# Linear attention and a gated layer on one core: tiles for the group sums, and the block-diagonal product in two halves

## The chip, the cores and the metric

The kernel runs on one core of a Trainium2 chip. The metric is the time of one execution on the device in microseconds. The engines are named as in the profile: PE is TensorE (its weight loads are PEld), DVE is VectorE, ACT is ScalarE, POOL is GpSimd, SP is SyncE, which issues nearly all transfers.

## The reference

```python
# q, k, v: (8, 8, 576, 64); w_in: (512, 2048); w_out: (2048, 512)
kv = np.einsum('bhsd,bhse->bhde', k, v)
out = np.einsum('bhsd,bhde->bhse', q, kv)
rms = np.sqrt(np.mean(out * out, axis=-1, keepdims=True) + 1e-06)
x = out / rms * g_norm                      # then to (4608, 512)
h = x @ w_in
sp = np.maximum(h, 0.0) + np.log1p(np.exp(-np.abs(h)))
g = h * erf(sp)
y = g @ w_out                               # (4608, 512) float32
```

## The kernel before

**Groups, batches, units.** The 4608 tokens are handled in nine groups. Groups 0 to 7 take the first 512 of the 576 rows of one batch element each; the remaining 64 rows of all eight elements are gathered in `x_last` and make group 8. In a group `x` is held transposed (features on the partitions, 512 tokens along the free dimension). The 2048 hidden features are cut into 16 units of 128; four units are a batch (`BATCH`), so a group has four batches and batch m of the whole kernel belongs to group m // 4. For each unit `hidden` makes `h`, ScalarE takes Softplus and Erf of it, VectorE multiplies, and the product with `w_out` is summed over the units into four tiles of sums, `e`.

**Two ways of multiplying.** Groups 0 and 1 use plain fp32 matmuls (L691 for `h`, L520 for the output) for most of their units. From group 2 on (`FIRST` = 2) each operand is cut into fp32r parts, and a product is twelve fp32r matmuls into two PSUM tiles, `n_ps` (eight) and `m_ps` (four), in `product` (L462). Their results are joined when they are evicted: L834 and L445 for `h`, L440 or L775 and L445 for `e`. The parts of the weights are written to DRAM once, in group 1, and read back for each group, as `w_in_parts` and `w_out_parts` (L595).

**Attention in pieces.** While one group goes through the gated layer, the attention of the next is made, one pair of heads (`p`) in each batch, in six pieces with fixed places in the batch's order:

- `products`: the two heads' `kv` products and the transposes of `q` (L297, L305, L319), copies of the two diagonal blocks into `bd_kv` (L312), of the tail of `q` into `qT_last` (L315, for two pairs at once, so only where `p` is even) and of `qT` (L320)
- `apply`: the block-diagonal product, for the tail of 64 tokens into a corner of the `kv` bank (L324) and for the 512 tokens into `se_ps` (L325); the tail's result goes to `x_last` (L326); Square (L328)
- `halve` and `mean`: the squares are cut into two fp32r parts (L338, L339), and two matmuls with `mean_w` give the means (L346, L347); then Ln, Exp, Square on ScalarE (L358 to L360)
- `norm`: three operations on VectorE (L366, L369, L378), the last of which writes `x` and is the last reader of the product's bank; `split` cuts `x` into `x_forms` (L405, L408, L411)

The engines run each their own queue in the order in which the program issues the instructions (`manual_schedule`); a tile taken from a pool waits for the last user of the buffer that it takes. In the main loop (from batch 8 on) the pieces stand at `places = (0, 2, 3, 5, 6, 8)`: before unit 0, after units 1 and 2, after results 0, 1 and 3 of the batch before. Batch m computes its own `h` and the results (`result`) of batch m - 1. SP's order in a batch is `FETCH`: one or two loads of parts at each place, between them the loads of `q`, `k`, `v` and, at the end of a group, the four stores of the sums (L531).

**Buffers that the change touches.** The pool `wide` has two buffers, and these take them in turns, in this order: xT of group 0, xT of group 1, `x_high` and `x_both` of group 1, the sums of group 1 (L735), and then `h` of every batch from 8 on (L822). The pool `acc` has one, for the sums of group 0, `old_h` of group 1's last four units (L700), and the sums of groups 2 to 8 (L773). In PSUM eight banks are split into `ps_h` (two), `ps_o` (four) and `ps_at` (two); the attention takes its tiles of one bank from `ps_at`.

Of the kernel before, what the change touches and what calls it, by code (L numbers as in the profile page):

```python
# [60 lines left out]
def kernel(  # L61
# [25 lines left out]
    attp = ctx.enter_context(tc.tile_pool(name="attp", bufs=1))  # L87
    dram = ctx.enter_context(tc.tile_pool(name="dram", bufs=1, space=bass.MemoryType.DRAM))

    wide = ctx.enter_context(tc.tile_pool(name="wide", bufs=2, side="right"))  # L90

    room, early_room, low_room = (ctx.enter_context(ExitStack()) for _ in range(3))
    first_w = room.enter_context(tc.tile_pool(name="first_w", bufs=1, side="right"))
    gate = room.enter_context(tc.tile_pool(name="gate", bufs=7, side="right"))
    early = early_room.enter_context(tc.tile_pool(name="early", bufs=2))
    ps_at = ctx.enter_context(tc.tile_pool(name="ps_at", bufs=2, space=PSUM))
    ps_h = ctx.enter_context(tc.tile_pool(name="ps_h", bufs=2, space=PSUM))
    ps_o = ctx.enter_context(tc.tile_pool(name="ps_o", bufs=1, space=PSUM))

    ctx.enter_context(tc.manual_schedule())  # L100

# [167 lines left out]
    def attention(T, p, pools=None):  # L269

        st = {}

        halves = FIRST <= T < B
        bd = bd_kv[:, (T * NP + p) % 2, :]

        q_tail, o_tail = slice(P, 2 * P), slice(2 * P, 2 * P + R)

        def bank(name):
            pool, tag = (pools or {}).get(name, (ps_at, "at"))
            return pool.tile([P, G], FP32, name=name, tag=tag)  # L280

        def square_tile(name):

            if T == 0:
                return gate.tile([P, G], FP32, name=name, tag="h")
            return attp.tile([P, G], FP32, name=name, tag="qT")

        def products():

            kv_ps = st["kv"] = bank("kv_ps")  # L290
            ks, vs, qs = (x.pop((T, p)) for x in (k_sb, v_sb, q_sb))
            C = chunks(T)
            for c in range(C):
                rows = slice(0, S // C + (c < S % C))
                for i in range(2):
                    s = slice(i * D, i * D + D)
                    nc.tensor.matmul(  # L297
                        kv_ps[s, s],
                        lhsT=ks[rows, i, c],
                        rhs=vs[rows, i, c],  # L300
                        start=(c == 0),
                        stop=(c == C - 1),
                    )
            if p % 2 == 0:
                nc.tensor.transpose(kv_ps[:, q_tail], q_last[:, p // 2], ident)  # L305
            if p == NP - 2:
                for i in range(NP):
                    load_last(T + 1, i)
            st["qT"] = square_tile("qT")
            for i in range(2):  # L310
                s = slice(i * D, i * D + D)
                nc.vector.tensor_copy(out=bd[s, s], in_=kv_ps[s, s])  # L312
            if p % 2 == 0:
                tails[T] = attp.tile([P, P], FP32, name="qT_last", tag="t")
                nc.vector.tensor_copy(out=tails[T], in_=kv_ps[:, q_tail])  # L315
            st["tail"] = tails[T][:, p % 2 * R : p % 2 * R + R]
            qt_ps = bank("qt_ps")
            for j in range(J):
                nc.tensor.transpose(qt_ps[:, j * P : j * P + P], qs[:, j], ident)  # L319
            nc.scalar.copy(st["qT"], qt_ps)  # L320

        def apply():
            qT, o_ps, kv_ps = st["qT"], bank("se_ps"), st.pop("kv")
            nc.tensor.matmul(kv_ps[:, o_tail], lhsT=bd, rhs=st.pop("tail"), start=True, stop=True)  # L324
            nc.tensor.matmul(o_ps, lhsT=bd, rhs=qT, start=True, stop=True)  # L325
            nc.vector.tensor_copy(out=x_last[:, p, T * R : T * R + R], in_=kv_ps[:, o_tail])  # L326
            st["o"] = o_ps
            nc.scalar.activation(qT, o_ps, AF.Square)  # L328

        def square():  # L330
            st["o"], st["qT"] = x_last[:, p, :], square_tile("sq")
            nc.scalar.activation(st["qT"], st["o"], AF.Square)

        def halve():
            sq = st.pop("qT")
            hi = st["hi"] = attp.tile([P, G], FP32R, name="sq_hi", tag="rms_r")
            lo = st["lo"] = attp.tile([P, G], FP32R, name="sq_lo", tag="sq_lo")
            nc.vector.tensor_copy(out=hi, in_=sq)  # L338
            nc.vector.tensor_tensor(out=lo, in0=sq, in1=hi.bitcast(FP32), op=ALU.subtract)  # L339

        def mean(table=True):
            ms = st["ms"] = bank("ms_ps")
            if halves:


                nc.tensor.matmul(ms, lhsT=mean_w, rhs=st.pop("hi"), start=True, stop=False)  # L346
                nc.tensor.matmul(ms, lhsT=mean_w, rhs=st.pop("lo"), start=False, stop=True)  # L347
                u = square_tile("u")
            else:
                u = st.pop("qT")  # L350
                nc.tensor.matmul(ms, lhsT=mean_w.bitcast(FP32), rhs=u, start=True, stop=True)  # L351
            if T > 0:
                r = attp.tile([P, G], FP32, name="rms_r", tag="rms_r")
                exp_ln_table()
            else:
                r = gate.tile([P, G], FP32, name="rms_r", tag="s")
            st["u"], st["r"] = u, r
            nc.scalar.activation(r, ms, AF.Ln, bias=eps_col)  # L358
            nc.scalar.activation(r, r, AF.Exp, scale=-0.5)
            nc.scalar.activation(u, r, AF.Square)  # L360
            if table and (T > 0 or p == NP - 1):
                softplus_table()

        def norm():
            ms, u, r = (st.pop(name) for name in ("ms", "u", "r"))
            nc.vector.scalar_tensor_tensor(  # L366
                out=u, in0=ms, scalar=EPS, in1=u, op0=ALU.add, op1=ALU.mult
            )
            nc.vector.scalar_tensor_tensor(  # L369
                out=u, in0=u, scalar=3.0, in1=r, op0=ALU.subtract, op1=ALU.mult  # L370
            )
            if T < FIRST:
                if T not in xT:
                    xT[T] = wide.tile([P, KC, G], FP32, name="xT", tag="h")
                x = xT[T][:, p, :]
            else:
                x = st["x"] = x_new.tile([P, G], FP32, name="x", tag="x")
            nc.vector.scalar_tensor_tensor(  # L378
                out=x,
                in0=st.pop("o"),  # L380
                scalar=gm_col,
                in1=u,
                op0=ALU.mult,
                op1=ALU.mult,
            )

        def split():
            if T >= FIRST:
                thirds(st.pop("x"), *(form[:, p] for form in x_forms[T]))

        def loads():
            load_pair(T * NP + p + 2)

        if T == 0:
            return products, apply, halve, mean, norm
        if T == B:
            return lambda: None, square, lambda: None, mean, norm, split

        pieces = ((products,), (apply,), (halve, loads)) if halves else ((products, loads), (apply,), ())
        return (*(partial(chain, *group) for group in pieces), mean, norm, split)  # L400


# [241 lines left out]
    for n in range(FIRST * FC + 1):  # L644
        T, f = divmod(n, FC)
        if n == FC:
            early_room.close()
            late = ctx.enter_context(tc.tile_pool(name="late", bufs=1))
            x_new = ctx.enter_context(tc.tile_pool(name="x_new", bufs=1))
            acc = ctx.enter_context(tc.tile_pool(name="acc", bufs=1))  # L650
            w_in_p = ctx.enter_context(tc.tile_pool(name="w_in_p", bufs=BATCH))
            low = low_room.enter_context(tc.tile_pool(name="low", bufs=1))
            forms = late.tile([P, 3, KC, G], FP32R, name="x_forms0")
            x_forms[FIRST] = [forms[:, i] for i in range(3)]
# [13 lines left out]
            gates(done)  # L668
        if T == FIRST - 1:
            if f == 0:  # L670
                x_high = wide.tile([P, KC, G], FP32R, name="x_high", tag="h")
                x_low = low.tile([P, KC, G], FP32R, name="x_low")
                for i in range(0, KC, 2):
                    upper(xT[T][:, i : i + 2], x_high[:, i : i + 2])
# [23 lines left out]
        if T < FIRST:  # L698
# [8 lines left out]
                add(h, m_ps)  # L707
            if T == FIRST - 1:
                if f == 1:
                    x_both = wide.tile([P, KC, G], FP32R, name="x_both", tag="h")  # L710
                    for i in range(0, KC, 2):
                        both_only(x_high[:, i : i + 2], x_low[:, i : i + 2], x_both[:, i : i + 2])
                    x_forms[T] = x_high, x_low, x_both
# [16 lines left out]
        if n >= LAG:  # L730
# [1 line left out]
            last = n - LAG in (FC - 1, whole - 1)  # L732
            project(f2, hs[n - LAG], last)
            if last:
                sums(*((acc, "e") if T2 < FIRST - 1 else (wide, "h")))  # L735
                if T2 == 0:
                    for j in range(J):
                        store(T2, j, es.pop(j))
# [26 lines left out]
    def result(T, b, j, g, w):  # L765
# [4 lines left out]
        )  # L770
        if b == 0:
            if j == 0:
                all_e = acc.tile([P, J, DM], FP32, name="e", tag="e")  # L773
                es.update((i, all_e[:, i]) for i in range(J))
            nc.vector.tensor_scalar(  # L775
                out=es[j], in0=ps[0], scalar1=SHIFT - 1.0, scalar2=None, op0=ALU.mult
# [9 lines left out]
    for m in range(first_batch, batches + 1):  # L786
# [32 lines left out]
        g, done = g_next, len(g_next)  # L819
        g_next = []  # L820
        if m < batches:
            h = wide.tile([P, BATCH, G], FP32, name="h", tag="h")  # L822
            s = gate_r.tile([P, BATCH, G], FP32, name="s", tag="s")
        for i in range(BATCH):
            if m < batches:
# [68 lines left out]
```

## Time and profile before

| | |
|---|---|
| Median of 12 runs | 953.72 us (951.44 to 954.97) |
| The profiled execution | 953.61 us, its span 951.8 us |
| Granted TensorE clock, mean | 0.998 |
| PE busy | 929.3 us (98%), 4272 matmuls |
| DVE busy | 740.8 us (78%) |
| ACT busy | 616.1 us (65%) |
| DMA | 259.78 MB, 273 GB/s over the span |

The shares are of the span. The first 150 us hold the conversion of the weights and group 0, the next 105 us group 1; from 256 us on the main loop runs, 28 batches of about 25 us and a last round of results. The times in the views are microseconds from the start of the span.

### The profile page before, as it was taken

To read this page: it belongs to the slowest core of one execution; us is meant where nothing else is said; L and a number is where in the kernel's file an instruction comes from. 1 tells how busy PE (TensorE), PEld (TensorE's weight loads), DVE (VectorE), ACT (ScalarE), POOL (GpSimd) and SP (SyncE) were. 2 spreads that over 40 slices of the span, in tenths; PEclk is the share of its full clock that TensorE was granted. 3 is DMA by queue.
4 is the path that set the end of the run, shared out by engine and by line. 5 is a ranking of instruction groups with operands and counts; after the bars stand their busy time and mean duration, and the time that the engine had idled before them with its cause. 6 is when DMAs were issued, how large, how long until landed. Compare 5 with 4: busy or idle time off the path is not lost.

```text
span 951.8 us, 11746 instructions
## 1 busy us (share of the span) xinstructions
PE 929.3 (98%) x4272; PEld 684.7 (72%) x4272; DVE 740.8 (78%) x1054; ACT 616.1 (65%) x825; POOL 2.4 (0%) x10
## 2 busy tenths in 40 slices
PE   6999999999998999999999999999999999999998
PEld 4444445665686788888888888888888788878886
DVE  3979958888575888888888887887887877777667
ACT  3889876777665666666666666666666666665552
POOL 1000000000000000000000000000000000000000
PEclk9999999999999999999999999999999999999999
DMA  9756505899699878898889889988896778768872
GB/s 256 278 167 214 163 6 219 308 351 336 209 360 334 286 266 300 290 305 295 299 312 314 290 294 307 329 291 285 286 338 254 262 255 346 285 249 310 331 272 64
DMA packets 111842, 259.78 MB, mean 273 GB/s; under 512 B 43864, under 2 KB 69544, under 8 KB 111784
## 3 DMA queue, kind: packets, MB, share of 16 engines
q1 hardware_dynamic: 110152, 256.73, 77.7%
q10 hardware_dynamic: 1568, 2.29, 0.8%
q8 instruction: 34, 0.56, 0.2%
q14 instruction: 24, 0.20, 0.1%
q0 software_dynamic: 64, 0.00, 0.0%
HBM read 224.40 MB, written 34.60 MB: 272 GB/s over the span
## 4 chain that ended last, share of the span: by engine, by line
PE 84%; ACT 6%; DVE 6%; DMA 3%; issue 1%; SPq 0%; DVEq 0%
PE n_ps L462 43%; PE m_ps L462 21%; PE o_ps L520 8%; PE h_ps L691 3%; PE se_ps L325 3%; PE kv_ps L297 2%; PE qt_ps L319 2%; DMA out_dram<-e 1%; DMA w_in_parts<-w_in 1%; ACT w_e L215 1%; ACT L103 1%; DVE h L445 1%; ACT w_m L219 1%; DMA v_sb<-in_v_dram 1%; PE ms_ps L351 1%
## 5 line engine op out<-in xcount | busy, mean ns | idle before, releaser
L462 PE MATMUL n_ps<-x_forms,w_in_parts 128*128 128x512 f32 x896 | 234.8, 404 | 4.8 <-ACT h L834 3.3
L462 PE MATMUL n_ps<-w_out_parts,g_forms 128*128 128x512 f32 x928 | 231.3, 391 | 0.0
L462 PEld LDWEIGHTS n_ps<-x_forms,w_in_parts 128*128 128x128 f32 x896 | 167.5, 189 | 49.2 <-issue 9.6
L462 PEld LDWEIGHTS n_ps<-w_out_parts,g_forms 128*128 128x128 f32 x928 | 174.2, 188 | 38.4 <-issue 1.4
L836 ACT ACTIVATE s<-h 128x512 f32<-128x512 f32 x112 | 71.1, 635 | 180.8 <-DVE h L445 180.8
L445 DVE TENSOR_TENSOR h<-m_ps,h 128x512 f32<-128x512 f32 x116 | 79.9, 688 | 68.1 <-ACT h L834 48.7
L462 PE MATMUL m_ps<-w_out_parts,g_forms 128*128 128x512 f32 x464 | 124.2, 389 | 0.0
L462 PE MATMUL m_ps<-x_forms,w_in_parts 128*128 128x512 f32 x448 | 120.2, 390 | 0.0
L520 PE MATMUL o_ps<-w_out_sb,h_sb 128*128 128x512 f32 x224 | 100.8, 592 | 0.3 <-DVE h_sb L642 0.3
L462 PEld LDWEIGHTS m_ps<-w_out_parts,g_forms 128*128 128x128 f32 x464 | 87.1, 188 | 18.1
L462 PEld LDWEIGHTS m_ps<-x_forms,w_in_parts 128*128 128x128 f32 x448 | 84.4, 188 | 17.8
L445 DVE TENSOR_TENSOR e<-m_ps,e 128x512 f32<-128x512 f32 x116 | 80.3, 692 | 17.9 <-PE m_ps L462 10.5
L440 DVE SCALAR_TENSOR_TENSOR e<-n_ps,e 128x512 f32<-128x512 f32 x88 | 60.4, 686 | 37.5 <-PE n_ps L462 37.5
L520 PEld LDWEIGHTS o_ps<-w_out_sb,h_sb 128*128 128x128 f32 x224 | 42.3, 190 | 48.9 <-issue 46.6
L834 ACT ACTIVATE h<-n_ps 128x512 f32<-128x512 f32 x112 | 65.6, 586 | 13.3 <-DMA w_in_parts<-w_in 9.4
L411 DVE SCALAR_TENSOR_TENSOR g_forms<-g_forms 128x1024 fp32r<-128x1024 f32 x58 | 71.1, 1226 | 2.0
L408 DVE TENSOR_TENSOR g_forms<-h,g_forms 128x1024 fp32r<-128x1024 f32 x58 | 70.6, 1218 | 1.7 <-ACT g_forms L405 1.4
L405 ACT ACTIVATE g_forms<-h 128x1024 fp32r<-128x1024 f32 x58 | 58.9, 1060 | 12.4 <-PE m_ps L462 9.8
L854 DVE TENSOR_TENSOR h<-h,s 128x1024 f32<-128x1024 f32 x56 | 66.0, 1219 | 0.7 <-ACT s L840 0.7
L691 PE MATMUL h_ps<-xT,w_in_sb 128*128 128x512 f32 x144 | 65.0, 595 | 0.8 <-DVE w_in_sb L240 0.6
L106 ACT ACT_TABLE_LOAD x44 | 56.5, 1283 | 0.7
L840 ACT ACTIVATE s<-s 128x1024 f32<-128x1024 f32 x56 | 56.3, 1052 | 0.3
(98 smaller groups left out, 1015.3 us busy)
## 6 DMA issues: line engine op xcount, KB each, us to landing
w_out_parts<-w_out SPq DMA_DIRECT2D x116, 768.0 KB
w_in_parts<-w_in SPq DMA_DIRECT2D x112, 768.0 KB
w_in<-w_new SPq DMA_DIRECT2D x16, 768.0 KB
q_sb<-in_q_dram SPq DMA_DIRECT2D x32, 256.0 KB
w_raw<-in_moe_w_out_dram SPq DMA_DIRECT2D x8, 1024.0 KB
out_dram<-e SPq DMA_DIRECT2D x32, 256.0 KB
k_sb<-in_k_dram SPq DMA_DIRECT2D x28, 287.5 KB
v_sb<-in_v_dram SPq DMA_DIRECT2D x28, 287.5 KB
```

Of the source, the lines that this page charges most:

```text
L106: nc.scalar.preload_act_table_set("softplus")
L405: nc.scalar.activation(high, x, AF.Copy, scale=1.0 + 2.0**-13)
L408: nc.vector.tensor_tensor(out=low, in0=x, in1=high.bitcast(FP32), op=ALU.subtract)
L411: nc.vector.scalar_tensor_tensor(out=both, in0=low.bitcast(FP32), scalar=SHIFT, in1=high.bitcast(FP32), op0=ALU.mult, op1=ALU.add,)
L440: nc.vector.scalar_tensor_tensor(out=out_, in0=ps, scalar=scale, in1=out_, op0=ALU.mult, op1=ALU.add)
L445: nc.vector.tensor_tensor(out=out_, in0=ps, in1=out_, op=ALU.add)
L462: nc.tensor.matmul(ps, lhsT=weights(form, k), rhs=moving(form, k), start=(form == forms[0] and k == 0), stop=(form == forms[-1] and k == 3),)
L520: nc.tensor.matmul(o_ps[j], lhsT=g[:, j * P : j * P + P], rhs=w_out_sb[:, f, :], start=(f == 0), stop=last,)
L691: nc.tensor.matmul(plain[i], lhsT=w_in_sb[:, c, i % FC * P : i % FC * P + P], rhs=xT[T][:, c, :], start=(c == 0), stop=(c == KC - 1),)
L834: nc.scalar.activation(h[:, i], n_ps, AF.Copy, scale=SHIFT - 1.0)
L836: nc.scalar.activation(s[:, i], h[:, i], AF.Softplus)
L854: nc.vector.tensor_tensor(out=part(h, half), in0=part(h, half), in1=part(s, half), op=ALU.mult)
```

## The change

The two wide tiles now have a name each: "a" for xT of group 0, `x_high` and the sums of groups 1 to 8, "b" for xT of group 1, `x_both` and `h` of the even batches from 8 on. `h` of the odd batches takes the tile of `acc`. The attention pieces of group 2 and later get one PSUM tile of two banks (`ps_two`, where `ps_at` was). The tail of `q` is laid beside `qT`, so that each of two halves has 256 + 32 columns, and the block-diagonal product becomes two matmuls of 288 columns, one in each bank; the means take the columns from 256 on of both banks, in four matmuls of 256 columns. The transposes of `q` are issued ahead of the copies.

```diff
-    wide = ctx.enter_context(tc.tile_pool(name="wide", bufs=2, side="right"))
+    wide = ctx.enter_context(tc.tile_pool(name="wide", bufs=1, side="right"))
...
         def bank(name):
+            if T >= FIRST:
+                return two_banks()[:, name in ("qt_ps", "se_ps")]
...
+        def two_banks():
+            if "two" not in st:
+                st["two"] = ps_two.tile([P, 2, G], FP32, name="at_ps", tag="at")
+            return st["two"]
+        HG, HR = G // 2, R // 2
+        def twofold(x):
+            return x.rearrange("p (i n) -> p i n", i=2) if halves else x
...
+            t = attp.tile([P, 2, HG + HR], FP32, name=name, tag="qT")
+            if tail:
+                return t
+            return t[:, :, :HG] if halves else t.rearrange("p i n -> p (i n)")[:, :G]
...
+            qt_ps = bank("qt_ps")
+            for j in range(J):
+                nc.tensor.transpose(qt_ps[:, j * P : j * P + P], qs[:, j], ident)
             if p == NP - 2:
                 for i in range(NP):
                     load_last(T + 1, i)
-            st["qT"] = square_tile("qT")
+            st["qT"] = square_tile("qT", halves)
             for i in range(2):
                 s = slice(i * D, i * D + D)
                 nc.vector.tensor_copy(out=bd[s, s], in_=kv_ps[s, s])
-            if p % 2 == 0:
-                tails[T] = attp.tile([P, P], FP32, name="qT_last", tag="t")
-                nc.vector.tensor_copy(out=tails[T], in_=kv_ps[:, q_tail])
-            st["tail"] = tails[T][:, p % 2 * R : p % 2 * R + R]
...
-            nc.scalar.copy(st["qT"], qt_ps)
+            if halves:
+                tail = tails.pop(T) if p % 2 else kv_ps[:, P : P + R]
+                nc.vector.tensor_copy(out=st["qT"][:, :, HG:], in_=twofold(tail))
+                if p % 2 == 0:
+                    tails[T] = attp.tile([P, R], FP32, name="qT_next", tag="t")
+                    nc.vector.tensor_copy(out=tails[T], in_=kv_ps[:, P + R : 2 * P])
...
+            if halves:
+                nc.scalar.copy(st["qT"][:, :, :HG], twofold(qt_ps))
...
         def apply():
+            if halves:
+                qT, two = st.pop("qT"), two_banks()
+                del st["kv"]
+                for i in range(2):
+                    nc.tensor.matmul(
+                        two[:, i, : HG + HR], lhsT=bd, rhs=qT[:, i], start=True, stop=True
+                    )
+                nc.vector.tensor_copy(
+                    out=twofold(x_last[:, p, T * R : T * R + R]), in_=two[:, :, HG : HG + HR]
+                )
+                o_ps = st["o"] = two[:, :, :HG]
+                qT = st["qT"] = qT[:, :, :HG]
+                nc.scalar.activation(qT, o_ps, AF.Square)
+                return
...
-            ms = st["ms"] = bank("ms_ps")
+            ms = st["ms"] = two_banks()[:, :, HG:] if halves else bank("ms_ps")
             if halves:
-                nc.tensor.matmul(ms, lhsT=mean_w, rhs=st.pop("hi"), start=True, stop=False)
-                nc.tensor.matmul(ms, lhsT=mean_w, rhs=st.pop("lo"), start=False, stop=True)
+                hi, lo = (twofold(st.pop(name)) for name in ("hi", "lo"))
+                for i in range(2):
+                    nc.tensor.matmul(ms[:, i], lhsT=mean_w, rhs=hi[:, i], start=True, stop=False)
+                    nc.tensor.matmul(ms[:, i], lhsT=mean_w, rhs=lo[:, i], start=False, stop=True)
...
-                    xT[T] = wide.tile([P, KC, G], FP32, name="xT", tag="h")
+                    xT[T] = wide.tile([P, KC, G], FP32, name="xT", tag="ab"[T])
...
+            at_room.close()
+            ps_two = ctx.enter_context(tc.tile_pool(name="ps_two", bufs=1, space=PSUM))
...
-                x_high = wide.tile([P, KC, G], FP32R, name="x_high", tag="h")
+                x_high = wide.tile([P, KC, G], FP32R, name="x_high", tag="a")
...
-                    x_both = wide.tile([P, KC, G], FP32R, name="x_both", tag="h")
+                    x_both = wide.tile([P, KC, G], FP32R, name="x_both", tag="b")
...
-                sums(*((acc, "e") if T2 < FIRST - 1 else (wide, "h")))
+                sums(*((acc, "e") if T2 < FIRST - 1 else (wide, "a")))
...
-                all_e = acc.tile([P, J, DM], FP32, name="e", tag="e")
+                all_e = wide.tile([P, J, DM], FP32, name="e", tag="a")
...
-            h = wide.tile([P, BATCH, G], FP32, name="h", tag="h")
+            pool, tag = (acc, "e") if m % 2 else (wide, "b")
+            h = pool.tile([P, BATCH, G], FP32, name="h", tag=tag)
```

`halves` is true for groups 2 to 7. VectorE's and ScalarE's operations on `qT`, `hi`, `lo`, the means and `x` are the same in number and elements and go through `twofold` views of two runs of 256.

More of the change, by code (lines that the diff above doesn't have):

```diff
@@ L95 @@
     early = early_room.enter_context(tc.tile_pool(name="early", bufs=2))
-    ps_at = ctx.enter_context(tc.tile_pool(name="ps_at", bufs=2, space=PSUM))
     ps_h = ctx.enter_context(tc.tile_pool(name="ps_h", bufs=2, space=PSUM))
     ps_o = ctx.enter_context(tc.tile_pool(name="ps_o", bufs=1, space=PSUM))
+    at_room = ctx.enter_context(ExitStack())
+    ps_at = at_room.enter_context(tc.tile_pool(name="ps_at", bufs=2, space=PSUM))
     ctx.enter_context(tc.manual_schedule())
@@ L278, in bank, with square_tile @@
         def bank(name):
+            if T >= FIRST:
+                return two_banks()[:, name in ("qt_ps", "se_ps")]
             pool, tag = (pools or {}).get(name, (ps_at, "at"))
             return pool.tile([P, G], FP32, name=name, tag=tag)
-        def square_tile(name):
+        def two_banks():
[5 more added lines that the diff above has]
+            return x.rearrange("p (i n) -> p i n", i=2) if halves else x
+        def square_tile(name, tail=False):
             if T == 0:
                 return gate.tile([P, G], FP32, name=name, tag="h")
-            return attp.tile([P, G], FP32, name=name, tag="qT")
+            t = attp.tile([P, 2, HG + HR], FP32, name=name, tag="qT")
+            if tail:
+                return t
+            return t[:, :, :HG] if halves else t.rearrange("p i n -> p (i n)")[:, :G]
         def products():
@@ L312, in products @@
                 nc.vector.tensor_copy(out=bd[s, s], in_=kv_ps[s, s])
-            if p % 2 == 0:
-                tails[T] = attp.tile([P, P], FP32, name="qT_last", tag="t")
-                nc.vector.tensor_copy(out=tails[T], in_=kv_ps[:, q_tail])
-            st["tail"] = tails[T][:, p % 2 * R : p % 2 * R + R]
-            qt_ps = bank("qt_ps")
-            for j in range(J):
-                nc.tensor.transpose(qt_ps[:, j * P : j * P + P], qs[:, j], ident)
-            nc.scalar.copy(st["qT"], qt_ps)
-        def apply():
+            if halves:
[4 more added lines that the diff above has]
+                    nc.vector.tensor_copy(out=tails[T], in_=kv_ps[:, P + R : 2 * P])
+            else:
+                if p % 2 == 0:
+                    tails[T] = early.tile([P, P], FP32, name="qT_last", tag="t", bufs=1)
+                    nc.vector.tensor_copy(out=tails[T], in_=kv_ps[:, q_tail])
+                st["tail"] = tails[T][:, p % 2 * R : p % 2 * R + R]
+            if halves:
+                nc.scalar.copy(st["qT"][:, :, :HG], twofold(qt_ps))
+            else:
+                nc.scalar.copy(st["qT"], qt_ps)
+        def apply():
+            if halves:
[12 more added lines that the diff above has]
+                return
             qT, o_ps, kv_ps = st["qT"], bank("se_ps"), st.pop("kv")
@@ L337, in halve @@
             lo = st["lo"] = attp.tile([P, G], FP32R, name="sq_lo", tag="sq_lo")
-            nc.vector.tensor_copy(out=hi, in_=sq)
-            nc.vector.tensor_tensor(out=lo, in0=sq, in1=hi.bitcast(FP32), op=ALU.subtract)
+            nc.vector.tensor_copy(out=twofold(hi), in_=sq)
+            nc.vector.tensor_tensor(
+                out=twofold(lo), in0=sq, in1=twofold(hi.bitcast(FP32)), op=ALU.subtract
+            )
         def mean(table=True):
-            ms = st["ms"] = bank("ms_ps")
+            ms = st["ms"] = two_banks()[:, :, HG:] if halves else bank("ms_ps")
             if halves:
-                nc.tensor.matmul(ms, lhsT=mean_w, rhs=st.pop("hi"), start=True, stop=False)
-                nc.tensor.matmul(ms, lhsT=mean_w, rhs=st.pop("lo"), start=False, stop=True)
+                hi, lo = (twofold(st.pop(name)) for name in ("hi", "lo"))
+                for i in range(2):
+                    nc.tensor.matmul(ms[:, i], lhsT=mean_w, rhs=hi[:, i], start=True, stop=False)
+                    nc.tensor.matmul(ms[:, i], lhsT=mean_w, rhs=lo[:, i], start=False, stop=True)
                 u = square_tile("u")
@@ L352, in mean @@
             if T > 0:
-                r = attp.tile([P, G], FP32, name="rms_r", tag="rms_r")
+                r = twofold(attp.tile([P, G], FP32, name="rms_r", tag="rms_r"))
                 exp_ln_table()
@@ L378, in norm @@
             nc.vector.scalar_tensor_tensor(
-                out=x,
+                out=twofold(x),
                 in0=st.pop("o"),
```

## The prediction, before the run

> **What bounds the kernel now.** I read the page's busy shares first, then the chain that ended last, then the waits and the chain between 236 and 330 us, and last the timeline of VectorE beside TensorE over several batches.
>
> ```profile
> PE 929.3 (98%) x4272; PEld 684.7 (72%) x4272; DVE 740.8 (78%) x1054; ACT 616.1 (65%) x825; POOL 2.4 (0%) x10
> PE 84%; ACT 6%; DVE 6%; DMA 3%; issue 1%; SPq 0%; DVEq 0%
> ```
>
> TensorE is the bound: 98% busy, and 84% of the chain. A saving must shorten TensorE's own work or close one of its few gaps. The chain (start, length, what) shows one gap outside the start and the tail:
>
> ```profile
> 271.34 1.85 PE n_ps L462 x8
> 273.19 0.18 SPq L595
> ...
> 273.47 10.18 DMA out_dram<-e
> ...
> 283.71 9.07 DMA w_in_parts<-w_in
> 292.77 0.60 ACT h L834
> ```
>
> Here ScalarE's eviction of a new `h` (L834) waits until 292.77. The waits put it down to a weight load:
>
> ```profile
> ACT h L834 <- DMA w_in_parts<-w_in: 9.4, 1, 9.4
> ```
>
> That label cannot be the cause, since L834 reads only `n_ps`, finished about 10 us before. What L834 also needs is its tile. In order of allocation the two buffers of `wide` go xT0, xT1, x_high, x_both, then `e` of group 1 (L735), then `h` of batch 8, then `h` of batch 9: the last takes the buffer of group 1's sums and must wait for their four stores. The timeline has those issued at 273.47, 275.62, 280.61 and 282.77; the first landed 10.18 us after issue, and 282.77 plus 10.0 is 292.77. So the wait is the stores'. Its price is read by stretch (length; busy PE, PEld, DVE, ACT, POOL; clock; DMA share; GB/s):
>
> ```profile
> 286.00:292.00 6.00, 4.14 (x18) 2.78 (x16) 0.19 (x1) 0.00 (x0) 0.00 (x0) 1.00 1.02 422
> 292.00:298.00 6.00, 4.58 (x13) 3.63 (x14) 3.78 (x5) 2.60 (x5) 0.00 (x0) 0.72 0.67 217
> ```
>
> TensorE runs dry, and restarts at a granted clock of 0.72. In the chain batch 9 begins its first product at 280.83 and batch 10 at 311.60: 30.77 us. Later batches take 24.72 (311.60 to 336.32) and 24.83 (to 361.15) in turn, mean 24.78. The stall costs 30.77 - 24.78 = 6.0 us.
>
> How close are the other engines in the steady state? `x` (L378) closes the vector chain of an attention piece, and the next piece's first product waits for its buffers:
>
> ```profile
> 334.71 0.75 DVE L378 SCALAR_TENSOR_TENSOR x<-se_ps,gm_col,u 128x512 f32<-128x512 f32 x1
> 433.05 0.75 DVE L378 SCALAR_TENSOR_TENSOR x<-se_ps,gm_col,u 128x512 f32<-128x512 f32 x1
> 334.94 0.80 PE L297 MATMUL kv_ps<-v_sb,k_sb 116*64 116x64 f32 x20
> 434.06 0.80 PE L297 MATMUL kv_ps<-v_sb,k_sb 116*64 116x64 f32 x20
> ```
>
> After the stall `x` comes late (its end at 335.46 is past the start of `kv_ps`), then gains: its starts are 24.57, 24.52, 24.58 and 24.50 us apart up to 408.31. From 433.05 it moves in step with TensorE and ends 0.26 us before `kv_ps`. So the free loop of VectorE and ScalarE is 24.54 us, TensorE's is 24.78, and each batch has 0.24 us to spare.
>
> **What the Trainium skill says.** "TensorE: Matmul & The Clock Gate", Back-to-back issue gap, prices a warm matmul of N columns at N/2.4 + 2.5 ns, 216 ns at 512. The trace has 1.81 us for eight fp32r products (226 ns), near it, and 3.43 us for eight fp32 instructions (429 ns): an fp32 product here is two instructions of two passes each. The same page, LDWEIGHTS, gives 107 ns for 128 columns; four transposes with a weight load each take 0.44 us (110 ns), which agrees. "PSUM — Partial Sum Buffer", PSUM bank collisions, has two engines kept apart in a bank even at disjoint columns, two readers included; no run here shows a collision, but the new layout puts `o`, its tail and the means in the same two banks, so their users go one after the other. "VectorE: DVE Perf Modes", perf-mode tier table, allows fp32 copies 2x in SBUF and 1x from PSUM: the SBUF CAST of 512 columns takes 419 ns here, the other 512-column operations 690.
>
> **Part 1, the buffers: -6.0 us.** `h` of batch 9 goes to the former tile of the sums (`acc`, "e"), last held by `old_h`, whose last reader in batch 8, L408 at 261.34, ends 20 us before it is wanted. Even and odd batches then use two tiles in turns as before. The sums keep one tile. What is late next? Group 2's first sum (L775) now waits for group 1's stores, landed at 292.77; without the stall the results of batch 9 start at 280.83 + 11.8 = 292.6, and L775 comes after a 1.8 us product, at 294.5: 1.7 us to spare. The weights: between the first and the last landing (283.65 to 292.77) 3.75 MB went by, 411 GB/s. In order of issue the part for unit 3 of batch 9 (issued 276.05) lands at about 287.9 and is wanted at 290.1; the last `w_out` part (issued about 281.5) at 292.2, wanted at 294.0. Close, but in time. Loads for batch 10, issued by 298.1 with 10 us to land, are wanted from 312 on. I take the whole 6.0.
>
> **Part 2, TensorE: -1.4 us, of which I take half.** Before, the tail product (64 columns) and the main one take 0.17 + 0.91 = 1.08 us from 261.57 to 262.65. Two fp32 products of 288 columns are four instructions of 288/512 x 429 = 241 ns, 0.97, with a first load exposed up to 0.05: 0.99. Saving 0.09, from 0.06 to 0.11. The means become four fp32r matmuls of 256 columns for two of 512 (0.454). At the transposes' 110 to 120 ns each: 0.48, so +0.03; if each load of 188 ns (its row) had to pass alone, 0.80, so +0.35; no gain below 4 x 109 ns = 0.44. Net -0.06 an attention piece, 24 pieces, -1.4; ends -2.3 and +7.
>
> **Part 3, VectorE: +3.9 us of work, hidden.** An even piece copies its tail as two halves of 64 columns (2 x 216 ns, the `x_last` row) for one copy of 291; an odd one copies 64 columns from SBUF, 33 + 152 = 185 ns by the CAST's own split. Mean +0.163 us. It lies in the free loop, which becomes 24.54 + 0.16 = 24.70 beside TensorE's 24.78 - 0.06 = 24.72: level. That is why I take half of part 2. In the four pieces of group 1's stage VectorE is busy 11.6 of 12 us at worst; +0.65 us there is the upper end, nothing the lower. The copy to `x_last` moves behind both products, and Square (L328) behind it by the bank rule; at 469.21 that copy ends 0.45 us ahead of Square, so it costs nothing while that holds.
>
> **Part 4, waits that move.** All of a piece's PSUM is one tile, so the next `kv_ps` waits for `x` (L378), where it could start after L366. Behind it queue the transposes and all of the next batch on TensorE. In step `x` ends 0.26 us before: the path from result 1's last matmul (about 478.0) is 0.69 + 2.35 + 0.69 + 0.69 + 0.75 with short hand-overs, 5.3 us, beside two results of 2.72 on TensorE. Nothing is added on that path: 0. `q_last`'s loads are issued four transposes later (0.44 us) for use a batch away: 0. The new views (halves of 256) change no element count, and I price them at 0; up to 0.27 if the CAST lost its 2x mode.
>
> **Sum.** 953.61 (span 951.8 and 1.8 around it) - 6.0 - 0.7 = 946.9. The median, 953.72, is 0.1 above that execution: 947.0.
>
> **Rivals.** *A held copy.* VectorE's tail copy and ScalarE's `qT` copy now write interleaved columns of one tile. If they are ordered one after the other, ScalarE's copy (460.31) waits for VectorE, which reaches the tail only at 463.0, and ScalarE's next work, L405, with it, so that L408 starts 1.7 us later. For it: ScalarE is in order; against: the columns are disjoint. The loop becomes 26.4, +1.6 us over 20 batches, +33: 980. It decides from 0.3 us a batch up (6.0/20), the point where it eats the gain. *Transfers late.* The margins of part 1 are 1.4 to 2.2 us with DMA at 1.02 of its share; if landings slip by 3 to 5 us, that much comes back: 949 to 952. *Thin slack.* The CAST at 1x (+0.27) and some 20 ns on each of ten operations put the loop at 25.1, +0.35 over 20 batches: 954. *Loads not hidden* in the means: 953. *Not what it says*: if L834's wait were truly for weights, the buffers would give nothing: 953.
>
> **How the numbers follow.** Main case 0.72, 945.2 to 948.6. Transfers late 0.09, thin slack 0.07, loads exposed or wrong wait 0.06, held copy 0.06. About 2 us (0.2%) can be told from no change. Faster: main, most of late, some of thin, 0.81; same 0.08; slower 0.11. The range reaches from part 2's best end, 944.8, over the late transfers to 952.5.
>
> **What would show it.** Right: no L834 wait over 1 us near 283, batch 9 taking about 24.7, clock 1.00 throughout, `se_ps` at about 0.97 in the chain, batches of 24.7. Wrong: a TensorE wait for L775, stores or `w_out_parts` at 292 to 295; `qT`'s copy waiting for VectorE; batches over 24.9.

## The result: slower, and the profile after

The changed kernel takes 975.78 us (median of 8 runs) beside 954.02 (median of 32); the ratio is 1.0228, 95% interval 1.0219 to 1.0237. The forecast was 947.0, range 944.8 to 952.5: wrong in sign. The case that came true is the one that it gave 6 in 100, the held copy, at 980. Lines of the changed kernel are numbered anew, and in the runs below some are shifted again by the lines moved: L348 is the copy of `qT`, L335 the copies to `bd_kv`, L338 and L341 those of the tail, L453 and L456 the first two cuts of `g_forms`, L426 is `x`, L316 the `kv` products, L357 the block-diagonal product, L886 the eviction of `h`.

The page's busy shares and the chain by engine:

```profile
PE 926.7 (95%) x4320; PEld 689.9 (71%) x4320; DVE 744.2 (76%) x1078; ACT 616.4 (63%) x825; POOL 2.4 (0%) x10
PE 84%; ACT 6%; DVE 5%; issue 3%; DMA 2%; SPq 0%; DVEq 0%
```

TensorE has 2.6 us less work than before and the span is 22.4 us longer, so the loss is idle time. The old stall is gone: the same stretch as before, the first of the two shown there (columns as there), is now full at full clock.

```profile
286.00:292.00 6.00, 6.00 (x27) 4.88 (x27) 5.57 (x7) 2.29 (x5) 0.00 (x0) 1.00 1.02 422
```

What is new stands in the waits (who waits for whom: us in total, times, longest):

```profile
ACT qT L348 <- DVE qT_next L341: 43.6, 12, 4.3
...
ACT qT L348 <- DVE bd_kv L335: 41.0, 11, 3.9
...
DVE g_forms L456 <- ACT g_forms L453: 31.8, 21, 1.7
...
PE at_ps L316 <- issue: 26.7, 18, 1.6
```

ScalarE's copy of `qT` waits for VectorE in 23 of 24 pieces. In the kernel before it waited for the transposes alone and ended well before VectorE came to `bd_kv`:

```profile
460.31 0.59 ACT L320 COPY qT<-qt_ps 128x512 f32<-128x512 f32 x1 [1.13 <-PE qt_ps L319]
...
462.55 0.45 DVE L312 COPY bd_kv<-kv_ps 64x64 f32<-64x64 f32 x2
```

The timeline of one batch of the changed kernel whose `p` is odd shows how the wait reaches TensorE (start, length, engine, line; in brackets the idle time before and its releaser):

```profile
436.07 0.75 DVE L426 SCALAR_TENSOR_TENSOR x<-at_ps,gm_col,u 128x512 f32<-128x512 f32 x1
...
436.92 0.80 PE L316 MATMUL at_ps<-v_sb,k_sb 116*64 116x64 f32 x20 [1.55 <-issue]
...
440.85 0.45 DVE L335 COPY bd_kv<-at_ps 64x64 f32<-64x64 f32 x2
...
441.33 0.20 DVE L338 COPY qT<-qT_next 128x64 f32<-128x64 f32 x1
441.39 0.59 ACT L348 COPY qT<-at_ps 128x512 f32<-128x512 f32 x1 [3.90 <-DVE bd_kv L335]
441.87 2.02 ACT L453 ACTIVATE g_forms<-h 128x1024 fp32r<-128x1024 f32 x2
...
442.97 1.23 DVE L456 TENSOR_TENSOR g_forms<-h,g_forms 128x1024 fp32r<-128x1024 f32 x1 [1.44 <-ACT g_forms L453]
```

VectorE reaches the `bd_kv` copies only after four additions to the sums and two cuts of `x`. ScalarE sits idle for 3.90 us with the transposes long done; L453 is queued behind its copy, L456 needs L453, and VectorE loses 1.44 us that it does not get back before `x`. The batch before had the same delay, and its end stands at the top of the view: TensorE starts its next `kv` products at 436.92, 0.10 us after the end of `x` at 436.82. The view calls the 1.55 us before them "issue". That they are a wait for `x`, the last reader of the tile, is read from the distance: it is 0.10 us in all 18 batches from 305.44 on.

The `kv` products' starts are 26.39 and 26.15 us apart in turns, mean 26.27 (18 intervals, 279.34 to 752.17: 472.83).

### The profile page after: what moved, and what is told of

Its sections match the earlier page's. It is cut to its first block, busy times and chain, and to the rows that moved or that the text cites. A ratio compares the mean times of both kernels' runs of the same rounds, so it can differ in the third digit from the quotient of the medians.

```text
span 974.2 us, 11965 instructions
## 1 busy us (share of the span) xinstructions
PE 926.7 (95%) x4320; PEld 689.9 (71%) x4320; DVE 744.2 (76%) x1078; ACT 616.4 (63%) x825; POOL 2.4 (0%) x10
## 4 chain that ended last, share of the span: by engine, by line
PE 84%; ACT 6%; DVE 5%; issue 3%; DMA 2%; SPq 0%; DVEq 0%
PE n_ps L510 43%; PE m_ps L510 22%; PE o_ps L568 8%; PE h_ps L741 3%; PE at_ps L357 2%; PE at_ps L316 2%; PE at_ps L328 1%; DMA w_raw<-in_moe_w_in_dram 1%; ACT w_e L217 1%; ACT L105 1%; DMA v_sb<-in_v_dram 1%; ACT w_m L221 1%; DVE h L493 1%; PE at_ps L395 1%; PE at_ps L394 1%
## 5 line engine op out<-in xcount | busy, mean ns | idle before, releaser
L510 PE MATMUL n_ps<-x_forms,w_in_parts 128*128 128x512 f32 x896 | 230.0, 398 | 3.0 <-DVE x_forms L456 1.6
L456 DVE TENSOR_TENSOR g_forms<-h,g_forms 128x1024 fp32r<-128x1024 f32 x58 | 70.7, 1219 | 31.8 <-ACT g_forms L453 31.8
L568 PEld LDWEIGHTS o_ps<-w_out_sb,h_sb 128*128 128x128 f32 x224 | 42.0, 190 | 47.1 <-issue 44.7
L886 ACT ACTIVATE h<-n_ps 128x512 f32<-128x512 f32 x112 | 65.5, 585 | 3.9 <-PE n_ps L510 3.7
L348 ACT COPY qT<-at_ps 128x512 f32<-128x512 f32 x24 | 14.1, 587 | 84.6 <-DVE qT_next L341 43.6
L453 ACT ACTIVATE g_forms<-h 128x1024 fp32r<-128x1024 f32 x58 | 58.7, 1056 | 12.4 <-PE m_ps L510 9.8
```

The source lines that it names most:

```text
L453: nc.scalar.activation(high, x, AF.Copy, scale=1.0 + 2.0**-13)
L456: nc.vector.tensor_tensor(out=low, in0=x, in1=high.bitcast(FP32), op=ALU.subtract)
L510: nc.tensor.matmul(ps, lhsT=weights(form, k), rhs=moving(form, k), start=(form == forms[0] and k == 0), stop=(form == forms[-1] and k == 3),)
L568: nc.tensor.matmul(o_ps[j], lhsT=g[:, j * P : j * P + P], rhs=w_out_sb[:, f, :], start=(f == 0), stop=last,)
L886: nc.scalar.activation(h[:, i], n_ps, AF.Copy, scale=SHIFT - 1.0)
```

## The experiments

Theory H: the order is kept between the two readers of the two-bank PSUM tile. ScalarE reads the second bank, VectorE the first, but both read one tile, and ScalarE's copy is issued after VectorE's. Rivals: Q, the order comes from the interleaved columns of `qT` in SBUF, as the prediction's rival had it; R, the buffers lengthen the batches; G, the other new work does; W, the wait of batch 9 was for weights. P, N, T and B, further below, are explained in the expectations.

**e1, the buffers alone.** Edit to the kernel before: only the pools and tags of `wide`, `acc`, `x_high`, `x_both`, `e` and `h` from the diff. 

> The kernel before with the buffers of the change alone (sums on tile a, h on tile b and the tile of acc in turns); the product as before. Theory H (the buffers close the stall of batch 9, and all of the loss comes from the product's part): 954.0 - 6.0 = 948, no L834 wait near 283 us, batch 9 at 24.8 us. Rival W (that wait was for weights): 954.

Measured 947.69 beside 953.87; ratio 0.9936 (0.9916 to 0.9956). H holds, W falls. There is no L835 wait (`h`'s eviction in this kernel) near 283, and `kv` starts at 281.57 and 306.29 make batch 9 24.72 us.

**e2, the product alone.** Edit to the changed kernel: the same lines back. 

> The changed kernel with the buffers of before (two of wide in turns, sums on acc). Theory H: batches of 26.3 us as in the changed kernel; batch 9 waits for the stores again until about 292.8, which hides its hold, so it takes 30.8 in place of 26.1: 975.8 + 4.7 = 980.5. Rival R (the buffers also cause part of the long batches): batches of 24.8 and about 954.

Measured 979.8; ratio 1.0275 (1.0251 to 1.0298). The loss is the product's. Batches take 26.40 and 26.15 us in turns, batch 9 30.04 us (279.13 to 309.17) instead of 26.1. Its waits between 260 and 320 us now name the stall's cause, which in the kernel before had to be inferred:

```profile
ACT h L885 <- DMA out_dram<-e: 4.9, 1, 4.9
```

**e3, ScalarE's copy first.**

```diff
             st["qT"] = square_tile("qT", halves)
+            if halves:
+                nc.scalar.copy(st["qT"][:, :, :HG], twofold(qt_ps))
...
-            if halves:
-                nc.scalar.copy(st["qT"][:, :, :HG], twofold(qt_ps))
```

> The changed kernel with ScalarE's copy of qT issued ahead of VectorE's copies of bd and the tail. Theory H (ScalarE's copy, a reader of the two-bank PSUM tile, is ordered behind VectorE's earlier readers of that tile, 3.9 to 4.3 us in the queue, and its next work with it): the hold goes, batches of 24.7, 947. Rival G (one tile for all, so that kv_ps waits for x, or two-run views, or more copies make the loop long whatever the order): batches stay above 26, 970 or more.

Measured 947.11; ratio 0.9930 (0.9912 to 0.9949). The views, the copies and the one tile are all still there, so G falls. Its timeline:

```profile
429.56 2.09 PE L510 MATMUL n_ps<-x_forms,w_in_parts 128*128 128x512 f32 x8
429.84 0.59 ACT L334 COPY qT<-at_ps 128x512 f32<-128x512 f32 x1 [1.02 <-PE at_ps L328]
...
432.19 0.45 DVE L339 COPY bd_kv<-at_ps 64x64 f32<-64x64 f32 x2
...
432.76 1.22 DVE L456 TENSOR_TENSOR g_forms<-h,g_forms 128x1024 fp32r<-128x1024 f32 x1
...
452.06 0.75 DVE L426 SCALAR_TENSOR_TENSOR x<-at_ps,gm_col,u 128x512 f32<-128x512 f32 x1
...
453.07 0.80 PE L316 MATMUL at_ps<-v_sb,k_sb 116*64 116x64 f32 x20
```

The copy now waits for the transposes alone and ends 1.8 us before VectorE comes to `bd_kv`; L456 follows at once; `x` ends 0.26 us ahead of the `kv` products. The order is still kept, only the other way round. In four pieces VectorE is the one that comes first, and now it waits for ScalarE:

```profile
DVE bd_kv L339 <- ACT qT L334: 6.8, 4, 2.5
```

**e4, the copy in the middle.** Edit: the same two lines, behind the `bd` copies and ahead of the tail copies. The copy is issued once in each piece, after both; the second copy in the text below was not in the kernel.

> The changed kernel with ScalarE's copy of qT issued between the two bd copies and the tail copies (inside the loop of two, so after the first bd copy, and a second time after the second). It is 24 copies more of 0.59 us on ScalarE. Theory H (order by the shared PSUM tile): the copy still waits for the bd copies; the even batches lose the wait for two tail copies (0.43 us each, 10 batches): 975.8 - 4 = 972, the odd ones stay at 26.1 to 26.4. Rival Q (order by the interleaved columns of qT in SBUF, as the prediction put its rival): the copy is ahead of the tail copy, so the hold is gone: 947 to 950.

Measured 974.22; ratio 1.0211 (1.0193 to 1.0228). This separates H from Q: the copy of `qT` now stands ahead of every writer of the interleaved columns and still waits as long, for copies that only share the PSUM tile with it. First its timeline, then its waits:

```profile
441.27 0.59 ACT L337 COPY qT<-at_ps 128x512 f32<-128x512 f32 x1 [3.90 <-DVE bd_kv L335]
```

```profile
ACT qT L337 <- DVE bd_kv L335: 78.0, 22, 3.9
```

The size agrees too. Even batches fell from 26.39 to 26.02 us (`x` at 305.60 and 331.62), near the 0.43 of the two tail copies; odd ones stayed at 26.14. The median fell by 1.6, less than the 4 expected. The loop did gain 3.3 us (`x` of batch 9 to `x` of batch 27: 469.56 for 472.88), but the `kv` products of batch 8 start 1.1 us later (255.69 for 254.57); the 2.2 left are about the difference of the two profiled executions (973.69 and 975.97).

**e5, e6, e7, the two halves without the hold.** e5 is the kernel of e3, e6 that of e1, e7 is e2 with ScalarE's copy first. All ran on one chip.

> The changed kernel with ScalarE's copy of qT first, once more with more rounds, beside the kernels that have one half of it each. Both theories below have 947.1, batches of 24.65 and 24.78 in turns.

> The buffers alone once more. Theory P (the product in halves is worth its TensorE time, 0.06 us in each of 20 batches): 1.3 us above the run with both, 948.4. Rival N (VectorE's added copies eat it): equal to the run with both, 947.1.

> The product's part alone with ScalarE's copy of qT first; buffers as before, so the stall of batch 9 is there. Theory P: 954.0 - 1.3 = 952.7. Rival N: 954.0. If the hold came from the buffers' part in any way, over 960.

Measured: e5 947.2, ratio 0.9925 (0.9912 to 0.9939); e6 948.12, ratio 0.9937 (0.9925 to 0.9950); e7 952.49, ratio 0.9984 (0.9976 to 0.9992), beside 954.33. So the product in halves is worth 1.8 us by e7 and 0.9 by e5 against e6, whose intervals overlap: theory P's 1.3 lies between, N falls by e7. The starts of the `kv` products show why the two figures differ. With ScalarE's copy first batch 8 starts 0.9 us later (255.38 in e5, 254.52 in e6); why was not followed. And e7's batch 10, after the stall, takes 24.8 us where that of the kernel before takes 25.5. The batches of e3, the same kernel as e5, measure the gain directly, here beside two of the kernel before (length first; lines of e3, then of before):

```profile
403.64:428.42 24.78, 24.78 (x131) 20.36 (x130) 20.13 (x31) 15.91 (x22) 0.00 (x0) 1.00 0.94 323
428.42:453.07 24.65, 24.65 (x130) 20.24 (x129) 20.05 (x30) 15.91 (x22) 0.00 (x0) 1.00 0.85 295
```

```profile
434.06:458.77 24.71, 24.71 (x127) 19.97 (x126) 19.93 (x29) 15.90 (x22) 0.00 (x0) 1.00 0.86 303
458.77:483.62 24.85, 24.85 (x129) 20.09 (x128) 20.07 (x30) 15.92 (x22) 0.00 (x0) 1.00 0.87 288
```

Mean 24.72 for 24.78, 0.06 us a batch, though DVE has 0.09 us more work in it. e5 is faster than the kernel before and than the changed one; beside the buffers alone its gain is not clear of the noise.

**e8, the transposes last.** Edit to the changed kernel: the three lines of `qt_ps` and its transposes moved behind VectorE's copies, ahead of ScalarE's.

> The changed kernel with the transposes of q issued after VectorE's copies, where the kernel before had them. Theory T (order is kept over the whole two-bank tile, so TensorE's write to the second bank waits for VectorE's reads of the first): TensorE idles from the kv products' end to the last copy, about 3.8 us in each of 20 batches, period 28.5: 1020 or more, with waits of the transposes for the copies of bd and of the tail. Rival B (order is kept for each bank, and the hold has another source): TensorE does not wait, 976.

Measured 1065.08 in one run. Theory T holds: TensorE's write to the second bank waits for VectorE's read of the first, behind the `bd` copies in the odd pieces and behind the last tail copy in the even ones. The `bd` copies and the transposes take plain slices of one bank each, so the order does not come from the two-run views.

```profile
445.94 1.12 PE L346 MATMUL at_ps<-ident,q_sb 128*128 128x128 f32 x4 [3.58 <-DVE qT_next L338]
446.70 3.76 PE L510 MATMUL n_ps<-x_forms,w_in_parts 128*128 128x512 f32 x8
```

The size was off by 45 us, and the clock explains it. The second line has eight products in 3.76 us that took 2.09 in e3. The same batch in three stretches, with the granted clock third from the end (columns as above):

```profile
442.36:444.04 1.68, 0.00 (x0) 0.00 (x0) 1.58 (x4) 0.00 (x0) 0.00 (x0) 1.00 0.90 362
444.04:450.86 6.82, 4.92 (x14) 4.07 (x15) 3.94 (x8) 2.85 (x4) 0.00 (x0) 0.50 0.26 84
450.86:472.95 22.09, 22.09 (x116) 17.96 (x114) 14.56 (x21) 13.51 (x18) 0.00 (x0) 1.00 0.85 283
```

From 140 us on TensorE idles 71.8 us in 21 stretches of over 2 us, and e5's 947.2 and this make 1019.0, near the 1020 expected. It is also busy for 89.3 us at half clock; half of that is lost, 44.7, and the estimate becomes 1063.7. So the order in which the change issues the transposes is needed by its shared tile; the copy of `qT` needed the same.

## Why the prediction was wrong, point by point

- **Part 1, the buffers, -6.0: right.** e1 gives -6.2 (953.87 to 947.69), e6 the same against its own before. The stores' release was read rightly against the trace's label (e2 names it), and the next transfers were in time: in e1 the first sum (L775) waited 0.57 us for a landing, but TensorE was not idle for 0.2 us at a time anywhere between 270 and 310.
- **Part 2, TensorE: right.** The chain of the changed kernel has the product at 0.97 us (0.99 in the sum) and the four mean matmuls at 0.12 each, 0.48. Net 0.06 us a batch, as priced, and loads of 188 ns did not have to pass alone. (The 110 ns that were said to agree with the page's price of a weight load are the spacing of the transposes in the chain; the loads' own rows last 141 ns in median there and 188 for the means.) The prediction took half of it, for VectorE's sake; in the two batches of e3 shown TensorE is busy throughout, so there the whole of it came. The low end of the range does not follow from the sum: 953.72 - 6.0 - 2.3 is 945.4, not 944.8.
- **Part 3, VectorE: right.** The copies take 225 + 215 and 196 ns for 216 twice and 185. The CAST keeps its 2x mode in the two-run view: 418 ns.
- **Part 4, waits that move: the step that failed.** It took the one tile's wait at `kv_ps` and priced it at 0, rightly, as e3 shows. It did not ask what else changes when two banks become one tile. The bank rule was applied to Square behind the copy to `x_last`, which do share banks, and not to the copy of `qT` behind the copies of `bd`, which share only the tile. The missing term is 26.27 - 24.72 = 1.55 us a batch. Over the 18 batches between the `kv` starts it makes 28.0 us; batch 28 is 1.6 longer too (24.69 us for e5's 23.07, between the first products of two batches), and the changed kernel reaches batch 9 0.8 us before e5 (279.34 and 280.14). Together 28.8 us, the difference of the two spans (974.2 and 945.4).
- **The held copy, right in its course and price, wrong in its cause and chance.** Its 1.6 us a batch is the measured 1.55, and its chain (ScalarE in order, L405 behind the copy, L408 late) is the trace's. But it tied the order to the columns of `qT` in SBUF and argued that they are disjoint. They are, and ScalarE did not wait for them: VectorE's copy into them at 441.33 is still running when ScalarE's starts at 441.39. That is the one argument given against the case, which got 6 in 100 and stayed out of the range. That the price fits is partly luck: in an odd piece VectorE reaches the `bd` copies, the true releaser, only 0.48 us before the tail (440.85 and 441.33), so either cause gives nearly the same wait. It had 20 batches where 19 are longer, hence 33 us for 29.6.
- **The profile's own sign** for this step ("`qT`'s copy waiting for VectorE", batches over 24.9) was named and came.

The Trainium skill, "PSUM — Partial Sum Buffer", PSUM bank collisions, tells of two engines in one bank, and says that the same pairs at different banks run clean. The order seen here goes across two banks: 3.90 us behind the `bd` copies. So the runs fit an order that the program's waits keep for the tile as a whole, and not one that the banks ask for. Whether the chip would need it within one tile, no run here shows. The kernel before, with a tile for each bank, has no such wait (460.31 on ScalarE, 462.55 on VectorE). The product in halves with two tiles of one bank, which would be the plainest test, was not run.

## What to carry to other kernels

When PSUM tiles are merged, list every pair of engines that touches the merged tile, and ask for each pair which instruction is issued first. In these runs the later one waited, even where both only read and at different banks. Then put first the one whose engine arrives first in the trace; here moving one line turned 975.8 us into 947.2. A label on a wait is the last arrival, not the cause: count what the waiting instruction needs, its tile's former user included.

## What the runs showed of the hardware that was not expected

Idle stretches of about 3.5 us, once in a batch, cost TensorE more than themselves. In e8 the granted clock fell to 0.50 while TensorE was still idle, 1.68 us after its last matmul in the batch shown, and stayed there for 6.82 us. It was low 19 times from 140 us on, fifteen times for 6.82 us and four times for 3.4; the shortest idle stretch in which it fell was 2.75 us (from 175.25). It did not fall each time: the stretches of 2.07 us from 262.25 and of 3.47 us from 780.20 left it at 1.00. Over the run e8's clock is 0.945, where every execution of the other kernels had 0.996 or more. In the changed kernel gaps of 1.4 to 1.56 us in 18 batches left it at 1.00. e8 is a single execution.
